# Attention weights kept in 32 bits and streamed past stationary values, two heads on the two halves of TensorE's columns

## Chip, cores and metric

One core of a Trainium2 chip. The metric is the device time of one execution, in microseconds (us). Shown for the kernel before are three runs and one profiled execution, which has a time of its own.

## What is computed

Clustered attention, then a mixture of experts. There are 4 batches, 8 heads, 768 positions, head size 64, 16 clusters per head. A query attends only to keys of its own cluster (if there is none, the row is uniform over all keys). The output of attention, 3072 tokens of 512, goes through 8 experts with hidden size 1024, whose gates are normalised over tokens and experts eight times.

```
mask   = argmax_c(q_n . c_n) == argmax_c(k_n . c_n)
scores = where(mask, q k^T / 8, -1e9)
attn   = exp(scores - max);  attn = attn / (sum(attn) + 1e-9)
x      = attn v                                 # 3072 x 512
out    = sum_e P[:, e] * (relu(x w1[e]) w2[e])  # P from x w_gate
```

## The kernel before

Attention comes first, for 32 heads in 16 pairs; the expert layers follow and take most of the time. Inside attention there is no fixed loop. Each piece of work is a generator (`load_pair`, `split_part`, `assign_pair`, `max_chunk`, `max_rows`, `exp_chunk`, `values`, `out_pair`, `out_batch`), which yields what it waits for (an event, or a token that stands for a buffer) and, before each operation, an engine and a planned cost in us. `Planner.run` (L123) picks at each step among the ready pieces by their earliest start and their urgency (`KEYS`, L385), and the order of instructions on every engine is thereby fixed when the program is built. Where a step gives two engines with costs, the planner picks one. An instruction that takes longer on the chip than planned delays what was put behind it on its engine.

A head is 768 keys by 768 queries, with the keys along the partitions, in nine chunks of 512 score columns (`CHUNKS`, L181): for each pair of key tiles two chunks of one key tile and 512 queries and one chunk of both key tiles and the last 256 queries.

- `split_part` (L555) and `assign_pair` (L591) transpose q and k of two heads on TensorE, split them in a high and a low part and work out the clusters; `place_pair` (L660) moves halves between partitions by DMA.
- `max_chunk` (L695): one matmul for a rough score of 512 columns into one of two PSUM banks (`max_ps`), and VectorE's maximum over it (L714), 9 a head. `max_rows` (L720) takes the maximum of a row, splits its negative in two fp32r parts on VectorE (L728 to L737), transposes them on TensorE (L741), and writes them by SP's DMAs as two rows beside q, from where the next matmul subtracts them; a third part, `nh`, marks rows that have no key.
- `exp_chunk` (L761): two matmuls give 512 score columns in one of three banks (`exp_ps`); ScalarE takes the exponential into `pe`, 32 bits (L794). `pe` is then split for the next product: a cast to f16 `ph` on ScalarE or VectorE (L798, L800), and the rest `pl = pe - ph` in f16, nearly always on GpSimd (L802).
- `load_group` (L451) loads the values of four heads. It finds their largest magnitude (L469 to L493), scales and splits them in f16 parts `vh` (with a column of ones) and `vl` (L503, L505), and sums them over all keys for the rows without a key (L518 to L541).
- `values` (L806), one head at a time: `ph` and `pl` are the stationary operand, 128x128, and the 64 or 65 columns of `vh`, `vl` are streamed. There are three matmuls for each key tile and query tile, 108 a head, and six with 2 rows for the rows without a key (L836). The output has queries on the partitions, and its 65th column is the denominator. Three VectorE steps normalise it (L843 to L851); the accumulator is one PSUM bank.
- `out_pair` (L860) transposes the output of two heads on TensorE (L872) and copies it with a scale on ScalarE (L876) into `xT`, the layout that the expert layers read. `out_batch` (L882) stores it and forms the gate logits in 32 bits on three column strips of TensorE (L901).

A plain fp32 matmul is recorded as two MATMULs (two passes); fp32r is one pass. The line that the change replaces in `values`:

```
nc.tensor.matmul(av[:, i, :], ph, vh[:, j, :], ...)
nc.tensor.matmul(av[:, i, 0:D], ph, vl[:, j, :], ...)
nc.tensor.matmul(av[:, i, :], pl, vh[:, j, :], ...)
```

Of the kernel before, what the change touches and what calls it, by code (L numbers as in the profile page):

```python
# [8 lines left out]
F32 = mybir.dt.float32  # L9
# [11 lines left out]
P = 128  # L21
# [131 lines left out]
def attn_moe_kernel(  # L153
# [23 lines left out]
    PB = 5  # L177
# [130 lines left out]
    with ExitStack() as actx:  # L308
# [5 lines left out]
        ps_s = actx.enter_context(tc.tile_pool(name="ps_s", bufs=3, space=PSUM))  # L314
# [44 lines left out]
        for nm, ts in bufs.items():  # L359
            if "X" in nm:  # L360
                for t in ts:
                    nc.gpsimd.memset(t[64:128, :].bitcast(F32), 1.0 if nm[0] == "k" else 0.0)
# [12 lines left out]
        for i in range(3):  # L375
            nc.vector.memset(mm[i].bitcast(F32), 0.0)
# [54 lines left out]
        t_x, t_s, t_m, t_v = Tokens(2), Tokens(3), Tokens(2), Tokens(1)  # L431
        t_nat, t_sc, t_pe, t_ph, t_nh, t_vn = Tokens(2), Tokens(1), Tokens(5), Tokens(PB), Tokens(3), Tokens(1)

# [17 lines left out]
        def load_group(n):  # L451
# [3 lines left out]
            if n >= 2 * G:  # L455
                yield ev["v", n - G - 1]
                yield ev["out", n // 2 - G + 1]
# [8 lines left out]
            am4 = sm.tile([P, G], F32, name="am4")  # L466
            for i in range(G):
                yield DVE, 0.469
                nc.vector.tensor_reduce(  # L469
                    out=am4[:, i : i + 1], in_=vn[:, i].rearrange("p t d -> p (t d)"), axis=AX, op=ALU.max, apply_absolute_value=True  # L470
                )
            yield DVE, 0.073
            am = sm.tile([P, 1], F32, name="am")
            nc.vector.tensor_reduce(out=am, in_=am4, axis=AX, op=ALU.max)
            yield t_x
            yield PE, 0.13, 0.107, 0.1
            ps = misc_tile()
            nc.tensor.transpose(out=ps[0:1, 0:P], in_=am, identity=ident)
            yield DVE, 0.198
            gm = sm.tile([1, 1], F32, name="gm")  # L480
            nc.vector.tensor_reduce(out=gm, in_=ps[0:1, 0:P], axis=AX, op=ALU.max)
            yield DVE, 0.069
            nc.vector.tensor_scalar(out=gm, in0=gm, scalar1=float(2.0**-100), scalar2=None, op0=ALU.max)
            yield DVE, 0.069
            nc.vector.tensor_single_scalar(out=gm.bitcast(I32), in_=gm.bitcast(I32), scalar=0x7F800000, op=ALU.bitwise_and)
            yield PE, 0.14, 0.053, 0.01
            nc.tensor.matmul(ps[:, 0:1], ones[0:1, :], gm, start=True, stop=True)
            yield DVE, 0.065
            vinv = sm.tile([P, 1], F32, name="vinv")
            nc.vector.tensor_scalar(out=vinv, in0=ps[:, 0:1], scalar1=float(2.0**-12), scalar2=None, op0=ALU.mult)  # L490
            vs = sm.tile([P, 1], F32, name="vs")
            yield DVE, 0.075
            nc.vector.reciprocal(vs, vinv)  # L493
            t_x.put(plan)
            if n:
                plan.now.key = urgency("vsplit", n)
            yield POOL, 0.106
            vh = work.tile([P, G, NT, D + 1], F16, name="vh")
            vl = work.tile([P, G, NT, D], F16, name="vl")
            nc.gpsimd.memset(vh[:, :, :, D : D + 1], 1.0)  # L500
            for i in range(G):
# [3 lines left out]
                nc.vector.scalar_tensor_tensor(  # L505
                    out=vl[:, i], in0=vn[:, i], scalar=vs, in1=vh[:, i, :, 0:D], op0=ALU.mult, op1=ALU.subtract
                )

            if n:
                plan.now.key = urgency("vsum", n)  # L510
            elif GATES[2]:
                yield ev["rows", 0]
            vsum = None
            for i in range(1, NT):
# [6 lines left out]
            t_vn.put(plan)  # L521
# [3 lines left out]
            nc.tensor.matmul(ps[0:2, 0 : G * D], ones[:, 0:2], vsum.rearrange("p h d -> p (h d)"), start=True, stop=True)  # L525
            yield DVE, 0.39
            ms = sm.tile([2, G, D], F32, name="ms", bufs=1)
            nc.vector.tensor_scalar(
                out=ms.rearrange("p h d -> p (h d)"), in0=ps[0:2, 0 : G * D], scalar1=vs[0:2, :], scalar2=1.0 / S, op0=ALU.mult, op1=ALU.mult
            )  # L530
            t_x.put(plan)
            yield DVE, 0.6
            mh = sm.tile([2, G, D], F16, name="mh", bufs=1)
            nc.vector.tensor_copy(mh, ms)
            mh2 = sm.tile([2, G, D], F32, name="mh2", bufs=1)
            nc.vector.tensor_scalar(out=mh2, in0=mh, scalar1=sgn, scalar2=None, op0=ALU.mult)
            yield DVE, 0.67
            ve = sm.tile([2, G, D + 1], F16, name="ve")
            nc.vector.scalar_tensor_tensor(out=ve[:, :, 0:D], in0=ms, scalar=row, in1=mh2, op0=ALU.mult, op1=ALU.add)
            for i in range(G):  # L540
                nc.vector.tensor_copy(ve[:, i, D : D + 1], first)  # L541
            t.update(vh=vh, vl=vl, ve=ve, vinv=vinv)
# [152 lines left out]
        def max_chunk(n, c):  # L695
# [7 lines left out]
            if n not in heads:  # L703
                heads[n] = dict(views(n), mr=sm.tile([P, NT, 2], F32, name="mr", bufs=3))
# [15 lines left out]
        def max_rows(n):  # L720
# [5 lines left out]
            nm = sm.tile([P, NT], F32, name="nm")  # L726
            mr = sm.tile([P, NT], F32, name="mr1")
            nc.vector.tensor_reduce(out=mr, in_=t["mr"], axis=AX, op=ALU.max)  # L728
            yield DVE, 0.072
            nc.vector.tensor_scalar(out=nm, in0=mr, scalar1=-BIG / 2, scalar2=-1.0, op0=ALU.max, op1=ALU.mult)  # L730
            yield DVE, 0.072
            nc.vector.tensor_copy(m_[:, 0:NT], nm)
            plan.now.engine = None
            yield DVE, 0.072
            nc.vector.tensor_scalar(out=m_[:, 2 * NT : 3 * NT], in0=mr, scalar1=-BIG / 2, scalar2=None, op0=ALU.is_lt)
            yield DVE, 0.075
            nc.vector.tensor_tensor(out=m_[:, NT : 2 * NT], in0=nm, in1=m_[:, 0:NT].bitcast(F32), op=ALU.subtract)  # L737
# [18 lines left out]
            t["nh"] = nh = sm.tile([2, S], F32, name="nh", bufs=3)  # L756
            for j in range(2):
                nc.sync.dma_start(out=nh[j : j + 1, :].rearrange("o (t p) -> o t p", p=P), in_=mt[2 * NT : 3 * NT, :])
            ev["nh", n].set(plan, plan.copied(0.02))

        def exp_chunk(n, c):  # L761

            u = c // 3
# [4 lines left out]
            if c % 3:  # L768
                yield ev["unit", n, u]
            else:  # L770
                yield t_ph
# [6 lines left out]
            if c % 3 == 0:  # L778
                t["ph", u] = work.tile([P, 2, S], F16, name="ph", bufs=PB)
                t["pl", u] = work.tile([P, 2, S], F16, name="pl", bufs=PB)  # L780
                ev["unit", n, u].set(plan)
# [24 lines left out]
        def values(n):  # L806
# [6 lines left out]
            for c in range(NCH):  # L813
                yield ev["p", n, c]
                if c == NCH - 2:
                    yield ev["nh", n]
# [520 lines left out]
```

## Time and profile before

| | |
|---|---|
| three runs, us | 2541.73, 2542.37, 2546.51 |
| the profiled execution, us | 2536.28 |
| its span, first to last instruction | 2534.5 |
| mean granted TensorE clock | 0.974 of full speed |
| busy over the span | TensorE 95%, VectorE 58%, ScalarE 37%, GpSimd 26% |

Busy shares over the span mix attention with the expert layers, so the trace is read by stretches. TensorE's records overlap, because matmuls are pipelined: the distance from one start to the next tells what a matmul occupies, not its duration. In the rows an arrow stands between a tile and what it is computed from, and "<-DVE mr L714" at the end of a row names what ended the idle time before it. DVE is VectorE, ACT ScalarE, POOL GpSimd, PE TensorE.

### The profile page before, as it was taken

How to read it: one execution, taken by the hardware profiler on the slowest of the kernel's cores; microseconds unless marked ns; L12 is line 12 of the kernel's file. 1: busy time of each engine (PE TensorE's matmuls, PEld its weight loads, DVE VectorE, ACT ScalarE, POOL GpSimd, SP SyncE). 2: the span in 40 equal slices, each digit the busy share in tenths (PEclk: the TensorE clock that was granted, in tenths of full speed). 3: DMA queues.
4: the chain of work that ended last, by engine and by line, in shares of the span. 5: the costliest groups of instructions: out<-in, count | busy, mean ns of one | idle time of the engine just before them, and what ended most of it. 6: DMA issues, size and time to landing. Idle time of an engine off the chain costs nothing.

```text
span 2534.5 us, 38588 instructions
## 1 busy us (share of the span) xinstructions
PE 2401.7 (95%) x15528; PEld 1371.1 (54%) x15528; DVE 1474.1 (58%) x2704; ACT 942.5 (37%) x1748; POOL 669.8 (26%) x583
## 2 busy tenths in 40 slices
PE   7988899887898999999999999999999999999999
PEld 4766677664444545455545455555555555555554
DVE  8999899998775554444444446544444434434444
ACT  5776677665424242424333322222222221221221
POOL 5777567665505050504232300000000000000000
PEclk8999899989898999999999999999999999999999
DMA  8454354416877453425243313332232222232332
GB/s 185 102 118 105 83 120 96 121 43 239 292 258 236 149 189 111 150 100 171 95 156 117 123 71 110 119 113 92 95 111 92 98 108 92 101 105 92 103 111 89
DMA packets 154708, 320.68 MB, mean 127 GB/s; under 512 B 61088, under 2 KB 90528, under 8 KB 154016
## 3 DMA queue, kind: packets, MB, share of 16 engines
q1 hardware_dynamic: 154528, 318.21, 39.9%
q8 instruction: 122, 2.00, 0.3%
q14 instruction: 58, 0.48, 0.1%
HBM read 230.74 MB, written 58.72 MB: 114 GB/s over the span
## 4 chain that ended last, share of the span: by engine, by line
PE 67%; DVE 16%; POOL 6%; DMA 5%; issue 4%; ACT 2%; SPq 0%; POOLq 0%; ACTq 0%; DVEq 0%
PE h_ps L1140 28%; PE o_ps L1202 10%; PE o_ps L1203 10%; PE o_ps L1204 10%; DVE mr L714 4%; POOL r L1060 2%; DMA r<-in_moe_w 2%; DMA scan<-in_moe_w 2%; PE max_ps L710 2%; POOL wa L1072 1%; POOL wb L1069 1%; DVE am L286 1%; PE exp_ps L787 1%; PE av_ps L830 1%; PE exp_ps L788 1%
## 5 line engine op out<-in xcount | busy, mean ns | idle before, releaser
L1140 PEld LDWEIGHTS <-wa 128*128 128x128 f16 x5376 | 527.6, 98 | 468.4 <-issue 47.0
L1152 DVE SCALAR_TENSOR_TENSOR hl<-c,hh 128x384 f16<-128x384 f32 x512 | 316.8, 619 | 537.7 <-ACT hh L1151 537.2
L1140 PE MATMUL h_ps<-xsT,wa 128*128 128x384 f16 x3072 | 586.1, 327 | 12.6 <-DVE u L1162 6.0
L1204 PE MATMUL o_ps<-wb,hl 128*128 128x512 f16 x1536 | 583.6, 380 | 7.7 <-DVE hl L1152 7.7
L1151 ACT ACTIVATE hh<-c 128x384 f16<-128x384 f32 x512 | 267.0, 522 | 857.4 <-DVE c L1162 853.7
L1202 PE MATMUL o_ps<-wb,hh 128*128 128x512 f16 x1536 | 584.3, 380 | 0.0
L1203 PE MATMUL o_ps<-wb,hh 128*128 128x512 f16 x1536 | 584.0, 380 | 0.0
L1140 PE MATMUL h_ps<-xsB,wa 128*128 128x384 f16 x2304 | 424.2, 328 | 17.0 <-DVE c L1162 14.9
L802 POOL TENSOR_TENSOR pl<-pe,ph 128x512 f16<-128x512 f32 x270 | 337.1, 1269 | 155.3 <-ACT ph L800 86.9
L1204 PEld LDWEIGHTS <-hl 128*128 128x128 f16 x1536 | 150.7, 98 | 189.1 <-DVE hl L1152 9.6
L1162 DVE SCALAR_TENSOR_TENSOR c<-h_ps,u 128x384 f32<-128x384 f32 x256 | 141.9, 554 | 181.8 <-PE h_ps L1140 180.8
L1162 DVE SCALAR_TENSOR_TENSOR u<-h_ps,m 128x384 f32<-128x384 f32 x256 | 141.8, 554 | 158.2 <-PE h_ps L1140 157.8
L1202 PEld LDWEIGHTS <-hh 128*128 128x128 f16 x1536 | 150.8, 98 | 141.1 <-issue 1.7
L1203 PEld LDWEIGHTS <-hh 128*128 128x128 f16 x1536 | 150.9, 98 | 140.2 <-issue 2.1
L1167 ACT ACTIVATE c<-h_ps 128x384 f32<-128x384 f32 x128 | 62.4, 488 | 414.1 <-PE h_ps L1140 414.0
L794 ACT ACTIVATE pe<-exp_ps 128x512 f32<-128x512 f32 x288 | 168.6, 600 | 92.7 <-PE exp_ps L788 85.9
L714 DVE TENSOR_REDUCE mr<-max_ps 128x1 f32<-128x512 f32 (+1 forms) x288 | 190.9, 677 | 16.9 <-PE max_ps L710 15.9
L710 PE MATMUL max_ps<-kX,qX 96*128 96x256 f32 (+1 forms) x384 | 130.3, 406 | 36.6 <-DVE mr L714 35.4
L1064 POOL TENSOR_TENSOR wa<-r,wa 128x256 f16<-128x256 f32 (+1 forms) x62 | 58.8, 967 | 393.6 <-ACT wa L1063 393.6
L1222 DVE SCALAR_TENSOR_TENSOR acc<-o_ps,gates,acc 128x512 f32<-128x512 f32 x168 | 125.3, 746 | 44.1 <-PE o_ps L1204 44.1
L800 ACT CAST ph<-pe 128x512 f16<-128x512 f32 x242 | 145.2, 623 | 2.6
L830 PE MATMUL av_ps<-vh,ph 128*128 128x65 f16 x1152 | 141.9, 200 | 4.1 <-DVE xn L851 4.1
(196 smaller groups left out, 2713.3 us busy)
## 6 DMA issues: line engine op xcount, KB each, us to landing
wa<-wd SPq DMA_DIRECT2D x96, 896.0 KB
wb<-wd SPq DMA_DIRECT2D x96, 512.0 KB
r<-in_moe_w SPq DMA_DIRECT2D x64, 512.0 KB
wd<-wa SPq DMA_DIRECT2D x32, 896.0 KB
scan<-in_moe_w SPq DMA_DIRECT2D x56, 512.0 KB
wd<-wb SPq DMA_DIRECT2D x32, 512.0 KB
qn<-in_q SPq DMA_DIRECT2D x16, 384.0 KB
kn<-in_k SPq DMA_DIRECT2D x16, 384.0 KB
```

What stands on the lines that cost most here:

```text
L710: nc.tensor.matmul(ps[:, y * (z - a) : (y + 1) * (z - a)], t["qa"][0:96, i * P : (i + 1) * P], t["k2"][0:96, a:z], start=True, stop=True)
L714: nc.vector.tensor_reduce(out=t["mr"][:, i0 : i0 + ni, ni - 1], in_=ps.rearrange("p (x c) -> p x c", x=ni), axis=AX, op=ALU.max)
L794: nc.scalar.activation(pe, ps.rearrange("p (x c) -> p x c", x=ni), AF.Exp, scale=SCALE)
L802: (nc.vector if e == DVE else nc.gpsimd).tensor_tensor(out=pl, in0=pe, in1=ph, op=ALU.subtract)
L830: nc.tensor.matmul(av[:, i, :], ph, vh[:, j, :], start=begin, stop=False, skip_group_check=True)
L1140: nc.tensor.matmul(ps[:, 0:HB], wa[:, w_, a, c, :], x[:, x_, c, :], start=(first and s_ == 0), stop=(s_ == len(steps) - 1), skip_group_che ...
L1151: nc.scalar.activation(hh[:, 2 - i, o], src, AF.Relu)
L1152: nc.vector.scalar_tensor_tensor(out=hl[:, 2 - i, o], in0=src, scalar=0.0, in1=hh[:, 2 - i, o], op0=ALU.max, op1=ALU.subtract)
L1162: nc.vector.scalar_tensor_tensor(out=t, in0=ps[:, 0:HB], scalar=KAPPA, in1=x, op0=ALU.mult, op1=ALU.add)
L1202: nc.tensor.matmul(po[i], hh[:, t, ti], wbh[:, t], start=(first and t == 0), stop=False)
L1203: nc.tensor.matmul(po[i], hh[:, t, ti], wbl[:, t], start=False, stop=False)
L1204: nc.tensor.matmul(po[i], hl[:, t, ti], wbh[:, t], start=False, stop=(last and t == 1))
```

## The change

The weights `pe` are no longer split. `values` works on a pair of heads: the stationary operand is a key tile of plain fp32 values, 128 keys by 64, and the weights move past it, 512 columns at a time. The first head's product lands in partitions 0 to 63 of the accumulator, the second's in 64 to 127, by way of the two halves of TensorE's columns. The output is therefore already transposed: `out_pair` goes. The denominator comes from sums of the weights over the key tiles, added on GpSimd or VectorE as the chunks appear (`t["sum"]`), and a matmul by ones that spreads the column sums over each head's 64 partitions; VectorE takes the reciprocal of 512 and 256 columns and multiplies. The accumulator takes two PSUM banks, still one buffer; the score banks go from three to two; the 32-bit weights have 14 buffers in place of 5 (the f16 parts had 5 of their own). The values' scale and f16 split go. The row steps behind the maximum move to one copy on ScalarE and two operations on GpSimd; the sign of the rows kept beside k changes with them. Constants and buffers are filled once at the start.

```diff
@@ buffers
-    PB = 5
+    PB = 14
-        ps_s = actx.enter_context(tc.tile_pool(name="ps_s", bufs=3, space=PSUM))
+        ps_s = actx.enter_context(tc.tile_pool(name="ps_s", bufs=2, space=PSUM))
-        t_x, t_s, t_m, t_v = Tokens(2), Tokens(3), Tokens(2), Tokens(1)
+        t_x, t_s, t_m, t_v = Tokens(2), Tokens(2), Tokens(2), Tokens(1)
...
@@ load_group
-            vn = nat.tile([P, G, NT, D], F32, name="vn", bufs=1)
+            vn = nat.tile([P, G, NT, D], F32, name="vn", bufs=2)
...
-            for i in range(G):
-                yield ACT, 0.507
-                nc.scalar.activation(vh[:, i, :, 0:D], vn[:, i], AF.Copy, scale=vs)
-                yield DVE, 0.529
-                nc.vector.scalar_tensor_tensor(
-                    out=vl[:, i], in0=vn[:, i], scalar=vs, in1=vh[:, i, :, 0:D], op0=ALU.mult, op1=ALU.subtract
-                )
...
@@ max_rows
-            nc.vector.tensor_scalar(out=nm, in0=mr, scalar1=-BIG / 2, scalar2=-1.0, op0=ALU.max, op1=ALU.mult)
-            nc.vector.tensor_copy(m_[:, 0:NT], nm)
-            nc.vector.tensor_scalar(out=m_[:, 2 * NT : 3 * NT], in0=mr, scalar1=-BIG / 2, scalar2=None, op0=ALU.is_lt)
-            nc.vector.tensor_tensor(out=m_[:, NT : 2 * NT], in0=nm, in1=m_[:, 0:NT].bitcast(F32), op=ALU.subtract)
+            yield ACT, 0.19
+            nc.scalar.copy(m_[:, 0:NT], mr)
+            yield POOL, 0.1
+            nc.gpsimd.tensor_scalar(out=m_[:, 2 * NT : 3 * NT], in0=mr, scalar1=-BIG / 2, scalar2=None, op0=ALU.is_le)
+            nc.gpsimd.tensor_tensor(out=m_[:, NT : 2 * NT], in0=mr, in1=m_[:, 0:NT].bitcast(F32), op=ALU.subtract)
...
@@ exp_chunk
-            if (yield (ACT, 0.52, RELUCT[0]), (DVE, 0.335, RELUCT[1])) == DVE:
-                nc.vector.tensor_copy(ph, pe)
-            else:
-                nc.scalar.copy(ph, pe)
-            e = yield ((DVE, 0.6, RELUCT[2]), (POOL, 1.113)) if n >= nheads - NL else (POOL, 1.113)
-            (nc.vector if e == DVE else nc.gpsimd).tensor_tensor(out=pl, in0=pe, in1=ph, op=ALU.subtract)
...
+            for part in parts:
+                if a not in old:
+                    old[a] = part
+                    continue
+                n_ = z - a
+                e = yield (POOL, 0.06 + n_ * 0.0023), (DVE, 0.08 + n_ * 0.00104, RELUCT[2])
+                (nc.gpsimd if e == POOL else nc.vector).tensor_tensor(out=st[:, a:z], in0=old[a], in1=part, op=ALU.add)
+                old[a] = st[:, a:z]
...
@@ values, for a pair p of heads
+            for c in range(NCH):
+                for x in range(2):
+                    yield ev["p", n + x, c]
+                yield PE, 0.87, 0.107, 0.43
+                if c == 0:
+                    av = ps_v.tile([P, 1024], F32, name="av_ps")
+                i0, ni, a, z = CHUNKS[c]
+                for i in range(i0, i0 + ni):
+                    for t, vn, o in two:
+                        nc.tensor.matmul(
+                            av[o, a:z], vn[:, i, :], heads[t]["pe", c][:, i - i0], start=(i == 0), stop=False, skip_group_check=True
+                        )
...
+            for a, z in SPANS:
+                nc.tensor.matmul(av[:, a:z], ve, nh[0:4, a:z], start=False, stop=True, skip_group_check=True)
...
+            for a, z in SPANS:
+                yield t_x
+                yield PE, (z - a) * 0.0021, 0.107, 0.11
+                ps = misc_tile()
+                for t, vn, o in two:
+                    nc.tensor.matmul(ps[o, 0 : z - a], ones[:, 0:D], heads[t]["sum"][:, a:z], start=True, stop=False, skip_group_check=True)
+                nc.tensor.matmul(
+                    ps[:, 0 : z - a], one5.rearrange("p x d -> p (x d)"), nh[:, a:z], start=False, stop=True, skip_group_check=True
+                )
+                yield DVE, 0.08 + (z - a) * 0.00104
+                ri = work.tile([P, z - a], F32, name="ri", bufs=2)
+                nc.vector.reciprocal(ri, ps[:, 0 : z - a])
+                t_x.put(plan)
+                yield DVE, 0.08 + (z - a) * 0.00104
+                nc.vector.tensor_tensor(out=xts[b][:, h // 2, a:z], in0=av[:, a:z], in1=ri, op=ALU.mult)
...
@@ order of the scores: the two heads of a pair in turn
-                plan.spawn(exp_chunk(n, c), urgency("exp", n, c))
+                plan.spawn(exp_chunk(n, c), urgency("exp", n // 2 * 2, 2 * c + n % 2))
```

## Rows read from the trace of the kernel before

Columns of the first group: stretch in us, its length, then busy us and instructions of TensorE, its weight loads, VectorE, ScalarE and GpSimd, TensorE's granted clock as a share of full speed, DMA share and GB/s. In a list by line: engine, operation, tiles, shapes and count, then busy us and mean ns, then the idle time before them and what ended it. In a timeline: start in us, duration in us, engine, line, operation.

**Rows 1.** Busy time by stretch, steady attention and the expert layers:
```profile
100.00:500.00 400.00, 357.48 (x4044) 277.68 (x4044) 374.53 (x758) 284.02 (x560) 265.50 (x228) 0.94 0.45 107
...
590.00:2534.00 1944.00, 1889.43 (x9996) 980.87 (x9995) 933.74 (x1627) 537.90 (x967) 282.64 (x242) 0.99 0.38 131
```

**Rows 2.** VectorE by line, 100 to 500 us:
```profile
L714 DVE TENSOR_REDUCE mr<-max_ps 128x1 f32<-128x512 f32 (+1 forms) x214 | 142.0, 677 | 12.9 <-PE max_ps L710 12.2
```

**Rows 3.** Timeline of TensorE, 330 to 338 us:
```profile
330.49 0.40 PE L787 MATMUL exp_ps<-qL,kH 128*128 128x512 f32 x1
330.73 0.40 PE L788 MATMUL exp_ps<-qX,kX 98*128 98x512 f32 x1
...
331.75 0.19 PE L830 MATMUL av_ps<-vh,ph 128*128 128x65 f16 x1
...
333.99 0.19 PE L832 MATMUL av_ps<-vh,pl 128*128 128x65 f16 x1
334.12 0.20 PE L836 MATMUL av_ps<-ve,nh 2*128 2x65 f16 x1
...
336.07 0.39 PE L787 MATMUL exp_ps<-qL,kH 128*128 128x256 f32 x1
```

**Rows 4.** Timeline of all engines, 300 to 308 us, a maximum on TensorE:
```profile
304.70 0.50 PE L710 MATMUL max_ps<-kX,qX 96*128 96x512 f32 x1 [2.61 <-DVE mr L714]
```

**Rows 5.** The same timeline, two additions on VectorE and GpSimd's work:
```profile
299.08 3.94 POOL L802 TENSOR_TENSOR pl<-pe,ph 128x512 f16<-128x512 f32 x3
...
300.62 1.39 DVE L518 TENSOR_TENSOR vsum<-vsum,vn 128x256 f32<-128x256 f32 x1
...
303.57 0.41 DVE L518 TENSOR_TENSOR vsum<-vsum,vn 128x256 f32<-128x256 f32 x1
```

**Rows 6.** VectorE by line and shape, 0 to 720 us, groups that go:
```profile
L798 DVE CAST ph<-pe 128x512 f16<-128x512 f32 x46 | 31.6, 689 | 3.1 <-ACT pe L794 3.1
...
L505 DVE SCALAR_TENSOR_TENSOR vl<-vn,vs,vh 128x384 f16<-128x384 f32 x32 | 23.1, 723 | 2.3 <-ACT vh L503 2.3
...
L802 DVE TENSOR_TENSOR pl<-pe,ph 128x512 f16<-128x512 f32 x18 | 20.2, 1138 | 0.1
L851 DVE TENSOR_TENSOR xn<-av_ps,rs 128x384 f32<-128x384 f32 x32 | 17.6, 550 | 0.4
L469 DVE TENSOR_REDUCE am<-vn 128x1 f32<-128x384 f32 x32 | 17.0, 538 | 0.0
L730 DVE TENSOR_SCALAR nm<-mr 128x6 f32<-128x6 f32 x32 | 15.1, 470 | 0.1
L737 DVE TENSOR_TENSOR mm<-nm,mm 128x6 fp32r<-128x6 f32 x32 | 13.9, 435 | 0.0
L732 DVE CAST mm<-nm 128x6 fp32r<-128x6 f32 x32 | 13.7, 428 | 0.0
```

**Rows 7.** The same view, reciprocals:
```profile
L845 DVE RECIPROCAL rs<-rs 128x6 f32<-128x6 f32 x32 | 5.9, 184 | 0.6
...
L1004 DVE RECIPROCAL rsum<-rsum 128x24 f32<-128x24 f32 x8 | 2.3, 293 | 0.1
```

**Rows 8.** Timeline of TensorE, 211 to 212.55 us, cluster scores:
```profile
211.85 0.51 PE L606 MATMUL misc_ps<-qn,cm 128*32 128x384 f32 x1
211.85 0.51 PE L606 MATMUL misc_ps<-kn,cm 128*32 128x384 f32 x1
...
212.19 0.49 PE L606 MATMUL misc_ps<-qn,cm 128*32 128x384 f32 x1
```

**Rows 9.** Timeline of TensorE, 212.5 to 214.8 us, gate scores:
```profile
212.52 1.90 PE L901 MATMUL misc_ps<-xT,wg 128*32 128x256 f32 x24
214.35 0.50 PE L710 MATMUL max_ps<-kX,qX 96*128 96x512 f32 x1
```

**Rows 10.** GpSimd and ScalarE by line and shape, 0 to 720 us:
```profile
L802 POOL TENSOR_TENSOR pl<-pe,ph 128x512 f16<-128x512 f32 x270 | 337.1, 1269 | 155.3 <-ACT ph L800 86.9 <-DVE ph L798 25.6 <-issue 19.4
...
L800 ACT CAST ph<-pe 128x512 f16<-128x512 f32 x242 | 145.2, 623 | 2.6
```

More of the change, by code (lines that the diff above doesn't have):

```diff
@@ L475, in load_group @@
[L475 to L496, printed above, removed]
@@ L509, in load_group @@
[L509 to L512, printed above, removed]
+            plan.now.key = urgency("vsum", n)
             vsum = None
@@ L520, in load_group @@
                 )
-            t_vn.put(plan)
             yield t_x
@@ L524, in load_group @@
             ps = misc_tile()
[L525 to L529, printed above, removed]
-            )
[L531 to L542, printed above, removed]
+            nc.tensor.matmul(ps[0:4, 0 : G * D], ones[:, 0:4], vsum.rearrange("p h d -> p (h d)"), start=True, stop=True)
+            yield DVE, 0.4
+            ms = sm.tile([4, G * D], F32, name="ms", bufs=1)
+            nc.vector.tensor_tensor(out=ms, in0=ps[0:4, 0 : G * D], in1=halves.rearrange("p h d -> p (h d)"), op=ALU.mult)
+            t_x.put(plan)
+            yield ACT, 0.4
+            mh = sm.tile([4, G * D], F32R, name="mh", bufs=1)
+            nc.scalar.copy(mh, ms)
+            yield DVE, 0.3
+            mh2 = sm.tile([4, G * D], F32, name="mh2", bufs=1)
+            nc.vector.tensor_scalar(out=mh2, in0=mh.bitcast(F32), scalar1=sgn4, scalar2=None, op0=ALU.mult)
+            yield DVE, 0.4
+            ve = sm.tile([4, G, D], F32R, name="ve")
+            nc.vector.scalar_tensor_tensor(
+                out=ve.rearrange("p h d -> p (h d)"), in0=ms, scalar=odd, in1=mh2, op0=ALU.mult, op1=ALU.add
+            )
+            t.update(vn=vn, ve=ve)
             ev["group", b, g].set(plan)
@@ L703, in max_chunk @@
             if n not in heads:
-                heads[n] = dict(views(n), mr=sm.tile([P, NT, 2], F32, name="mr", bufs=3))
+                heads[n] = dict(views(n), mr=mrs[n % 4])
             t = heads[n]
@@ L810, in values @@
             yield ev["group", b, h // G]
[L811 to L820 removed]
+            gr = groups[(b, h // G)]
@@ new lines, in values @@
+                plan.spawn(release(p, c), plan.now.key)
+            for x in range(2):
+                yield ev["nh", n + x]
+            yield PE, 0.34, 0.107, 0.11
+            for a, z in SPANS:
+                nc.tensor.matmul(av[:, a:z], ve, nh[0:4, a:z], start=False, stop=True, skip_group_check=True)
+            if h % G == G - 2:
+                t_vn.put(plan)
+            if h == 0:
+                if b:
+                    yield ev["batch", b - 1]
+                xts[b] = sm.tile([P, NC, S], F32, name="xT", bufs=1)
@@ L865, in out_pair @@
+            for x in range(2):
+                yield ev["s", n + x, NCH - 1]
             for a, z in SPANS:
                 yield t_x
-                yield PE, 0.12 * (z - a) / P, 0.107, 0.107
-                if h == 1 and a == 0:
-                    xts[b] = sm.tile([P, NC, S], F32, name="xT", bufs=1)
+                yield PE, (z - a) * 0.0021, 0.107, 0.11
                 ps = misc_tile()
-                for i in range(a // P, z // P):
-                    nc.tensor.transpose(out=ps[:, i * P - a : (i + 1) * P - a], in_=xn[:, i, :], identity=ident)
@@ L882, in out_batch @@
+            for x in range(2):
+                t_nh.put(plan)
+                t_sum.put(plan)
+                ev["v", n + x].set(plan)
+            t_v.put(plan)
+            if p + 1 < npairs:
+                plan.spawn(values(p + 1), urgency("values", 2 * p + 2))
+            if h == H - 2:
+                plan.spawn(out_batch(b), urgency("batch", n + 1))
+        xts = {}
         def out_batch(b):
```

152 lines of the change are left out of this document (56 added, 96 removed).

## The prediction

> **What bounds the kernel now.** I read the stretches first. The change touches only attention, the first 590 us of a span of 2534.5 us; the 1944 us behind it are the expert layers, which it leaves alone [rows 1]. Within attention the 400 us from 100 to 500 are steady: VectorE is busy 94%, TensorE 89%, ScalarE 71%, GpSimd 66%, and TensorE's granted clock averages 0.94 [rows 1]. The pace comes from the row maxima: one head has 9 of these reductions, a pair of heads 18, and 214 of them in 400 us are 11.9 pairs, so 33.6 us a pair [rows 2]. VectorE is at work 374.5 / 11.9 = 31.5 us of that.
>
> TensorE's 89% needs care, since matmul records overlap. Counted by starts, a 512-column matmul on fp32r data takes 0.24 us [rows 3]. A chunk needs one such matmul for the maximum and two for the scores: 18 x 0.72 = 13.0 us a pair. The values of one head are 108 weight loads of 128x128 f16, each with 64 or 65 columns, and 6 corrections; 96 of them and the corrections run from 331.75 to 336.07 [rows 3], 4.3 us, and with the other 12 it is 4.7, or 9.4 a pair. Six output transposes are some 0.7, and the transposes and cluster scores at the front of a pair about 3 (an estimate: 12 transposes at 0.12 from the 0.24 row, a cluster round of 0.67, the rest small). Sum 26.1 us: TensorE streams for 78% of the pace. What it loses is waiting, such as the 2.61 us before a maximum whose bank VectorE had not yet emptied [rows 4], and the lower of its two clock levels (1.2 GHz instead of 2.4), which the average of 0.94 contains. So **VectorE is the bound and TensorE follows.**
>
> VectorE is slow partly because of GpSimd: the same sum of values took 1.39 us while GpSimd was working through three subtractions, which end at 303.02, and 0.41 us after them, at 303.57 [rows 5]. Some of the groups below are slow for the same reason.
>
> **What leaves VectorE.** From [rows 6], whole attention: the f16 cast of weights 31.6, the weights' low parts 20.2, the values' low parts 23.1, the values' maxima 17.0, the normalisation 17.6, three of the small row steps 15.1 + 13.7 + 13.9; from [rows 7] the old reciprocals 5.9. Together 158 us, 9.9 a pair. A dozen smaller groups that go too are left as a margin.
>
> **What comes to VectorE.** The output is now transposed, so every one of the 64 lanes of a head holds the denominator of each query, and the reciprocal runs over 512 and 256 columns instead of 6. Does a reciprocal cost by its columns? 6 columns took 184 ns, 24 took 293 [rows 7]: (293 - 184) / 18 = 6.1 ns a column. 512 columns are then 3.3 us, 256 columns 1.7, 5.0 us a pair, or 80 us in all. The planner's costs in the diff are 0.61 and 0.35. The other bound, if the slope belonged to short operations alone, is 1.4 ns a column (550 ns for the 384 columns of the normalisation [rows 6]), 1.1 a pair; I take the slope, since it is measured on the same operation. The Trainium skill (VectorE: DVE Perf Modes, "First, the fixed hardware budget" and "Specifications") says that the divide repeats 8 times and that the clock is 0.96 GHz. An estimate by that page is 8.3 ns a column and 6.4 us a pair, which would make the sum 1.4 us a pair worse; no run here shows it. The slope above is the lower of the two, and it is the measured one. The new multiplications cost 2 x 0.55 = 1.1 a pair [rows 6]. The key-tile sums are 20 additions a pair, half of 512 and half of 256 columns; GpSimd's cost carries no penalty in the diff, and VectorE did 18 of 288 of the old subtractions [rows 6], so about 20 of 320, some 1 us each beside GpSimd, 1.3 a pair (bounds 0 and 4). The values' mean correction keeps about the same count of small operations. Sum 7.4.
>
> VectorE: 31.5 - 9.9 + 7.4 = **29.0 us a pair.**
>
> **TensorE.** Removed: 9.4 + 0.7 = 10.1. Added: per chunk, two heads times 512 columns of plain fp32, which goes in two passes. Do the halves of the columns run side by side? Products of 384 columns on neighbouring column strips start at the same 211.85, and the second passes 0.34 us later [rows 8]; 24 records, 12 products of 256 columns in threes, end before 214.35, so a round of three takes 0.43 [rows 9]. Strips do run together, and 512 columns cost 0.86 to 0.91; with 0.88, nine chunks are 7.9 a pair. Each change of the array's shape costs too: the 2-row correction starts 0.13 after its neighbour, where 75 matmuls of one shape before it start within 2.24 us, 0.03 apart [rows 3], and 0.11 passes after the strips [rows 9]. I take 0.1 a change; score matmuls stand between most chunks, so 9 x 2 x 0.1 = 1.8 (0 if all chunks came in runs). The correction: 768 columns of fp32r, 0.36, plus 0.2. The denominators: ones by the sums, 768 x 2 passes, 1.3, the 5-row term 0.36, and 0.6 for shapes. Sum 12.5. TensorE: 26.1 - 10.1 + 12.5 = **28.5 us a pair**, 2.4 more than before.
>
> **The others.** GpSimd's 337 us of subtractions [rows 10] turn into 160 additions of 512 columns and 160 of 256, at 1.27 and half of that about 306 us, less what VectorE takes, plus four small row operations a pair: unchanged, and it goes on holding up VectorE. ScalarE loses 145 us of casts [rows 10] and more; it has no part in the bound, so that gains nothing directly. Its new copies of the row maxima stand behind operations of 0.6 us [rows 10]; TensorE's transpose of them waits for ScalarE, then GpSimd, where it waited for VectorE. I cost that at nothing, because three slow VectorE steps go; if GpSimd's queue (1.27 us an entry) is ahead of the row, it is 1 to 2 us a pair. The score banks go from 3 to 2: with 0.5 us of matmul against 0.6 of exponential one bank fills while the other empties, nothing. The accumulator is one for two heads, and the next pair's values wait for sums, reciprocals and products: about 11 us (last additions 3, ones 1, reciprocals 5, products 1, handovers 1). Fourteen buffers of weights hold seven chunks of each head, and at some 1.8 us a chunk the scores can go on for 25 us, so this is hidden; with half the cover it would show. SP's queue gets the same transfers. Set-up adds about a dozen small fills and constants on VectorE before the first q arrives: hidden. At the start the first group's scale and split leave VectorE (about 5 us on the path); at the end the last pair's longer chain returns about 6.
>
> **The sum.** Before, the engine at the limit reached 31.5 / 33.6 = 94%. Now two engines stand at 29.0 and 28.5 in an order fixed in advance, so each delay of one idles the other; I take 92%: 29.0 / 0.92 = 31.5, that is 2.1 us a pair less, 34 us over 16 pairs. Against the profiled execution's 2536.3 us (span 2534.5 and 1.8 around it) that makes 2502, and I say **2501**. The median of the runs shown is 2542.4, 6 us above that execution; 0.2%, or 5 us, is about what a measurement of this kernel can tell from no change. At 96% it would be 30.2 a pair and 2482, at 90% 2514: this case's own range.
>
> **Rivals.**
> **More is gained.** Reciprocals at the rate of other operations (1.1 a pair, not 5.0) and no additions on VectorE give 29.0 - 3.9 - 1.3 = 23.8; then TensorE's 28.5, with half of the shape changes saved by runs 27.6, is the bound: 27.6 / 0.94 = 29.4, 67 us gained, 2469, and down to 2440 if the removed small groups and milder waits for GpSimd count. For it: VectorE's removed groups are certain. Against it: the slope. 0.26.
> **Slower: TensorE takes over and keeps its waits.** Now it loses 33.6 - 26.1 = 7.5 us a pair. A reciprocal of 3.3 us planned as 0.6 stands in front of the reductions that empty TensorE's banks, once a pair and then a shorter one, just where [rows 4] shows a wait. If the loss stays above 33.6 - 28.5 = 5.1 us, the kernel is slower; at 6.5 it is 35.0 a pair, 22 us more, 2558; if all 7.5 stay, 36.0 and 2574. Against it: most of those waits came from a VectorE that was full, and it has now 2.5 us less to do. 0.24.
> **The halves do not run together.** The chunks then take another 7.9 and the ones 1.3: 37.7 a pair, at 95% 39.7, 98 us more, 2634. Against it stand [rows 8, 9], so only 0.03. The Trainium skill (TensorE: Matmul & The Clock Gate, "Measured speedup vs the span model") gives 2.38-fold for three strips, not three; an estimate by that is 1.26 times the chunk's price, 2.3 us a pair or 37 us more, 2538. The rows here show no such loss.
> **Nothing measurable:** the efficiency falls to 86% and the gain goes. 0.07.
>
> **Numbers.** Forecast 0.40, more 0.26, slower 0.24 and 0.03, same 0.07: faster 0.66, same 0.07, slower 0.27. The range 2440 to 2562 leaves out the far ends of both rivals.
>
> **What the profile would show.** Reciprocals near 3.3 and 1.7 us; value matmuls of the two heads starting together, 0.43 to 0.45 apart by pass, and no weight casts on ScalarE; VectorE down to about 85 to 92% and TensorE's streaming up in the steady stretch; the expert stretch unchanged at 1944 us. Wrong would be: reciprocals near 0.7; the second head's products behind the first's; waits of the maxima for VectorE longer than now; a clock lower than 0.94.

## The result, and the profile after

The changed kernel takes 2567.9 us (median of 4 runs, 2566.9 to 2568.5), the kernel before 2543.1 in the same rounds: ratio 1.0095, interval 1.0078 to 1.0113. It is slower by 25 us, where 2501 us was forecast, about 42 less than the kernel before. The profiled execution's span is 2565.1 us, 30.6 more than before. All of it lies in attention: the expert layers still fill 1945 us.

Busy time by stretch of the changed kernel, columns as in [rows 1]:

```profile
100.00:500.00 400.00, 370.49 (x1886) 207.89 (x1884) 304.09 (x452) 173.11 (x347) 263.70 (x290) 0.92 0.43 101
...
620.00:2565.00 1945.00, 1890.05 (x9996) 980.76 (x9994) 935.17 (x1626) 541.49 (x972) 287.60 (x247) 0.99 0.38 131
```

VectorE is down from 94% to 76% of the steady stretch, ScalarE from 71% to 43%; TensorE is up from 89% to 93%, and its granted clock is down from 0.94 to 0.92. The maxima give the pace, as in [rows 2]. VectorE by line, 100 to 500 us, changed kernel:

```profile
L692 DVE TENSOR_REDUCE mrt<-max_ps 128x1 f32<-128x512 f32 (+1 forms) x202 | 133.7, 680 | 69.4 <-PE max_ps L688 68.6
```

202 / 18 = 11.2 pairs in 400 us, 35.6 us a pair instead of 33.6, and 16 times 2.0 us is about the 31 us of the span. VectorE now waits 68.6 us for TensorE's maxima, where it waited 12.2.

What came to VectorE, by line and shape, the attention stretch of the changed kernel (reciprocals, products, and the share of the key-tile sums that the planner gave it):

```profile
L836 DVE RECIPROCAL ri<-misc_ps 128x512 f32<-128x512 f32 x16 | 53.7, 3354 | 16.1 <-PE misc_ps L831 16.1
L836 DVE RECIPROCAL ri<-misc_ps 128x256 f32<-128x256 f32 x16 | 28.0, 1750 | 5.7 <-PE misc_ps L831 5.7
...
L839 DVE TENSOR_TENSOR xT<-av_ps,ri 128x512 f32<-128x512 f32 x16 | 10.9, 678 | 0.1
...
L777 DVE TENSOR_TENSOR psum<-psum,pe 128x256 f32<-128x256 f32 x10 | 9.8, 985 | 5.9 <-ACT pe L758 5.8
...
L777 DVE TENSOR_TENSOR psum<-psum,pe 128x512 f32<-128x512 f32 x9 | 7.9, 878 | 11.5 <-ACT pe L758 11.5
```

The end of a pair shows how a reciprocal gets in the way. Timelines of TensorE and VectorE in the changed kernel, 300 to 323 us:

```profile
301.31 1.08 PE L830 MATMUL misc_ps<-psum,ones 128*64 128x512 f32 x4
302.32 0.49 PE L831 MATMUL misc_ps<-nht,one 5*128 5x512 f32 x1
...
308.62 0.50 PE L688 MATMUL max_ps<-kX,qX 96*128 96x256 f32 x2 [0.36 <-DVE mrt L692]
...
311.75 1.08 PE L808 MATMUL av_ps<-pe,vn 128*64 128x512 f32 x4 [0.67 <-DVE xT L839]
...
314.92 0.50 PE L751 MATMUL exp_ps<-qL,kH 128*128 128x512 f32 x1
315.26 0.40 PE L752 MATMUL exp_ps<-qX,kX 98*128 98x512 f32 x1
...
321.56 1.08 PE L808 MATMUL av_ps<-pe,vn 128*64 128x512 f32 x4
322.57 0.38 PE L751 MATMUL exp_ps<-qL,kH 128*128 128x256 f32 x1
```

```profile
303.91 3.34 DVE L836 RECIPROCAL ri<-misc_ps 128x512 f32<-128x512 f32 x1
307.28 0.69 DVE L839 TENSOR_TENSOR xT<-av_ps,ri 128x512 f32<-128x512 f32 x1
307.89 1.28 DVE L692 TENSOR_REDUCE mrt<-max_ps 128x1 f32<-128x512 f32 x2
309.08 1.75 DVE L836 RECIPROCAL ri<-misc_ps 128x256 f32<-128x256 f32 x1
```

Between 303.91 and 307.89 no maximum is taken, and from 305.2 on, when the second of TensorE's two banks for them has been written, both stay full. The four passes of a chunk, two heads side by side, occupy 1.01 us (321.56 to 322.57): 0.86 of streaming and 0.15 for two changes of shape. The first score matmul behind such a change takes 0.34 (314.92 to 315.26) instead of the 0.24 of [rows 3].

At this pair end TensorE had other work and waited only 0.36 us for a maximum's bank. At others it stands still, here 2.70 us (363 to 369 us, TensorE and then VectorE):

```profile
365.16 0.33 PE L883 MATMUL misc_ps<-ident,gt 96*128 96x96 f32 x2
368.18 0.80 PE L688 MATMUL max_ps<-kX,qX 96*128 96x256 f32 x2 [2.70 <-DVE mrt L692]
```

```profile
364.22 3.36 DVE L836 RECIPROCAL ri<-misc_ps 128x512 f32<-128x512 f32 x1 [0.47 <-PE misc_ps L831]
367.50 0.63 DVE L692 TENSOR_REDUCE mrt<-max_ps 128x1 f32<-128x512 f32 x1
```

Between 100 and 500 us TensorE waits 13 times for a maximum, 18.5 us in all. In eight of these waits, 16.3 us, the bank comes free by the first maximum behind a reciprocal.

The clock falls at the same places. Of the 400 us, TensorE had 61 at the lower clock level, in nine spells at nine of the eleven pair ends. Each spell begins during or just behind a standstill of TensorE of 1.1 to 2.8 us: seven of these were waits for a maximum, one for the accumulator (L808) and one for a bank that a reciprocal reads (L238). The other two pair ends have standstills too (2.2 and 0.75 us) and no spell. The spell that follows the rows above, in the columns of [rows 1]:

```profile
368.20:371.60 3.40, 3.40 (x10) 2.57 (x10) 2.07 (x5) 1.33 (x3) 1.92 (x3) 0.50 0.00 0
```

**One account for all kernels.** The columns of the stretch 100 to 500 us give TensorE's budget. Pairs are maxima / 18 (in the table's order 214, 202, 219, 233, 206, 212, 207 and 221 maxima). Idle is 400 less TensorE's busy time. A granted share of 0.92 means that 8% of 400 us, 32 us of full-speed time, was lost to the lower of the two clock levels (1.2 and 2.4 GHz; a stretch at the lower one is granted 0.50). What is left, busy less clock loss, divided by the pairs, is what a pair needs of TensorE at full clock; the share is given to 0.01, so the need is known to about 0.2 us, and what the clock lost while TensorE was idle anyway is counted twice.

| kernel | pairs | idle, us | clock loss, us | need per pair, us |
|---|---|---|---|---|
| before | 11.9 | 42.5 | 24 | 28.0 |
| changed | 11.2 | 29.5 | 32 | 30.2 |
| one pass (e1) | 12.2 | 50.3 | 56 | 24.1 |
| no division (e2) | 12.9 | 8.8 | 0 | 30.2 |
| early free (e3) | 11.4 | 25.1 | 24 | 30.7 |
| true cost (e5) | 11.8 | 21.8 | 16 | 30.7 |
| runs of three (e7) | 11.5 | 38.8 | 32 | 28.6 |
| true cost and runs (e10) | 12.3 | 19.2 | 16 | 29.7 |

Before, a pair took 28.0 of need and 5.6 of loss (42.5 + 24 over 11.9). After, 30.2 of need and 5.5 of loss. **The work on TensorE grew by 2.2 us a pair and the loss did not shrink.** Its make-up changed: idle time went from 3.6 to 2.6 us a pair, and clock loss from 2.0 to 2.9. TensorE waits less for the maxima than before (28.5 us in this stretch then, 18.5 now), but most of what is left of them stands at the pair ends, where the clock falls. This row is of the kernel before, TensorE's waits in 100 to 500 us (total, times, longest):

```profile
PE max_ps L710 <- DVE mr L714: 28.5, 26, 4.7
```

The experiments ask where the need and the loss come from. The changed kernel ran only in its first rounds; the differences to it below are of medians. By the ratios to the kernel before, which ran in every round, some gains come out up to 5 us smaller: 26 us and not 29 for e5, 6 and not 9 or 10 for e6 and e7.

### The profile page after: what moved, and what is told of

Read it like the earlier page. It is cut to its first block, busy times and chain, and to the rows that moved or that the text cites. A ratio compares the mean times of both kernels' runs of the same rounds, so it can differ in the third digit from the quotient of the medians.

```text
span 2565.1 us, 32392 instructions
## 1 busy us (share of the span) xinstructions
PE 2438.1 (95%) x12720; PEld 1281.4 (50%) x12720; DVE 1401.9 (55%) x2349; ACT 807.5 (31%) x1493; POOL 674.8 (26%) x679
## 4 chain that ended last, share of the span: by engine, by line
PE 76%; DVE 9%; POOL 6%; issue 4%; DMA 3%; ACT 1%; SPq 0%; POOLq 0%; ACTq 0%; DVEq 0%
PE h_ps L1110 28%; PE o_ps L1174 11%; PE o_ps L1172 11%; PE o_ps L1173 11%; PE av_ps L808 5%; PE max_ps L688 3%; PE exp_ps L751 3%; DVE ri L836 2%; PE exp_ps L752 2%; POOL r L1030 2%; DMA r<-in_moe_w 2%; DVE mrt L692 2%; POOL wa L1042 2%; DVE am L286 1%; DMA scan<-in_moe_w 1%
## 5 line engine op out<-in xcount | busy, mean ns | idle before, releaser
L777 POOL TENSOR_TENSOR psum<-psum,pe 128x512 f32<-128x512 f32 (+1 forms) x237 | 251.5, 1071 | 123.1 <-ACT pe L758 116.4
L692 DVE TENSOR_REDUCE mrt<-max_ps 128x1 f32<-128x512 f32 (+1 forms) x288 | 189.8, 680 | 91.9 <-PE max_ps L688 91.0
L808 PE MATMUL av_ps<-pe,vn 128*64 128x512 f32 (+1 forms) x768 | 153.0, 510 | 8.8 <-DVE xT L839 8.8
L752 PE MATMUL exp_ps<-qX,kX 98*128 98x256 f32 (+1 forms) x384 | 134.5, 361 | 0.0
```

What stands on the lines that cost most here:

```text
L692: nc.vector.tensor_reduce(out=t["mr"][:, i0 : i0 + ni, ni - 1], in_=ps.rearrange("p (x c) -> p x c", x=ni), axis=AX, op=ALU.max)
L752: nc.tensor.matmul(o, t["k2"][0:98, ki], t["qa"][0:98, a:z], start=False, stop=True)
L777: (nc.gpsimd if e == POOL else nc.vector).tensor_tensor(out=st[:, a:z], in0=old[a], in1=part, op=ALU.add)
L808: nc.tensor.matmul(av[o, a:z], vn[:, i, :], heads[t]["pe", c][:, i - i0], start=(i == 0), stop=False, skip_group_check=True)
```

## The experiments

**e1, one pass.** Weights and values of the value product are read as bf16 through a view.

```diff
-    av[o, a:z], vn[:, i, :], heads[t]["pe", c][:, i - i0], ...
+    av[o, a:z], vn.bitcast(BF16).rearrange("p t (d u) -> p t d u", u=2)[:, i, :, 1],
+    heads[t]["pe", c].bitcast(BF16).rearrange("p n (s u) -> p n s u", u=2)[:, i - i0, :, 1], ...
```

> Leaves out the lower 16 bits of weights and values in the value product (both are read as bf16 through a view), so each product takes one pass instead of two; nothing else changes, and the planned costs stay, so the order does too. Theory A, TensorE's own work is the new bound (two passes, 0.86 us a chunk): 0.64 x 144 chunks = 92 us of TensorE go, and most of it shows, 60 to 90 us: 2478 to 2508. Theory B, the gap between two pairs (values stand still until sums, reciprocals and products have emptied the one accumulator): the gap of some 11 us a pair stays, only the dense part between gaps shrinks until VectorE or ScalarE binds: 20 to 50 us, 2518 to 2548.

Measured 2524.9 us, ratio to before 0.9929 (0.991 to 0.9948), so 43 us less than the changed kernel, inside the range of theory B; whether its gap is the accumulator's is asked by e3. Busy time by stretch of this kernel:

```profile
100.00:500.00 400.00, 349.75 (x1733) 209.72 (x1731) 338.22 (x490) 187.34 (x377) 285.94 (x315) 0.86 0.47 108
```

The need falls by 6.1 us a pair, as much as nine chunks at 0.64 (5.8) and the clock's rounding allow. (For 512 columns of both heads a recorded pass of plain fp32 occupies 0.43 us and the bf16 pass 0.22, so one pass in place of two takes away three quarters of the 0.86.) But idle and clock loss rise to 106 us, 8.7 a pair. Of 92 us of TensorE work that were taken away, about half came back as waiting and as lower clock: work alone is not what sets the pace.

**e2, no division.** `nc.vector.reciprocal(ri, ps)` becomes `nc.vector.tensor_copy(ri, ps)`.

> Leaves out the division: the reciprocal is replaced by a copy of the same shape, order unchanged. The reciprocals of 3.35 and 1.75 us become 0.7 and 0.4, 4.0 us a pair off VectorE, 64 us in all. Theory A: VectorE has slack (76% busy in the steady stretch), so under 10 us: 2558 to 2568. Theory B: the gap shrinks by 4 us in every pair and TensorE loses less to the low clock: 40 to 65 us, 2503 to 2528.

Measured 2501.4 us, ratio 0.9837 (0.9818 to 0.9855), 66 us less than the changed kernel: theory B, 2 us beyond its range, though what shrinks most is the wait for the maxima. Busy time by stretch, and who waited for whom on TensorE in 100 to 500 us, without the division:

```profile
100.00:500.00 400.00, 391.21 (x2126) 216.99 (x2124) 307.72 (x517) 197.37 (x397) 303.84 (x329) 1.00 0.47 110
```

```profile
PE misc_ps L714 <- POOL mm L710: 4.7, 5, 1.4
PE max_ps L688 <- DVE mrt L692: 3.1, 9, 0.8
```

The same view of the changed kernel:

```profile
PE max_ps L688 <- DVE mrt L692: 18.5, 13, 2.8
PE av_ps L808 <- DVE xT L839: 3.7, 3, 1.9
```

The waits of the maxima go from 18.5 us to 3.1, the clock stays at full but for one spell of 3.4 us, and the need is the same 30.2. So the division takes nearly the whole loss of a pair with it, although VectorE had a quarter of its time free. Here TensorE is busy 98% of the stretch, and a pair takes 30.9 us, close to the 30.2 that TensorE's work needs.

**e3, early free.** The accumulator is copied out at once and released.

```diff
+            ao = work.tile([P, S], F32, name="ao", bufs=1)
+            for a, z in SPANS:
+                yield ACT, 0.09 + (z - a) * 0.00098
+                nc.scalar.copy(ao[:, a:z], av[:, a:z])
+            t_v.put(plan)
+            if p + 1 < npairs:
+                plan.spawn(values(p + 1), urgency("values", 2 * p + 2))
```

> ScalarE copies the accumulator to SBUF (about 0.7 and 0.4 us) as soon as the last product is in, and the next pair's values may start; sums, reciprocals and the product follow from the copy. Nothing of the computation is left out. Theory A: TensorE's work is the same, so 0 to 10 us either way: 2558 to 2578. Theory B: the values no longer stand still at the end of a pair; TensorE is fed there and keeps its clock: 30 to 65 us less, 2503 to 2538, below the kernel before.

Measured 2562.7 us, ratio 1.0077 (1.0056 to 1.0098): 5 us less than the changed kernel. Theory B falls in the form in which I had it: TensorE no longer waits for the products (3.7 us before, none now), and the time hardly moves. TensorE's waits for VectorE, 100 to 500 us, early free:

```profile
PE max_ps L688 <- DVE mrt L692: 16.3, 12, 2.5
PE misc_ps L837 <- DVE ri L843: 3.0, 2, 1.5
```

The maxima still wait 16.3 us, 12.7 of them directly behind a reciprocal. What costs most is not the accumulator but what stands behind a reciprocal in VectorE's queue.

**e4, the row steps alone, on the kernel before.** `max_rows`, the sign of the rows and the prefilled maxima are taken from the change; the rest is the kernel before.

> The kernel before with one part of the change alone: the row steps behind the maximum move from VectorE (470 + 428 + 191 + 435 ns a head) to one ScalarE copy and two GpSimd operations. If VectorE bounds the kernel before, as its 94% says, 48 us of it go and 20 to 40 show: 2503 to 2523. If the longer way through ScalarE's and GpSimd's queues (entries of 0.6 and 1.3 us) delays the transpose of the rows, on which TensorE already waited 15.6 us, it is the same or up to 15 us slower: 2543 to 2558.

Measured 2550.4 us, ratio 1.0035 (1.0021 to 1.005). It is slower by 7 us in the median, but it doesn't answer the question, because the planner spent part of what was freed. VectorE by line, 100 to 500 us, this kernel:

```profile
L796 DVE CAST ph<-pe 128x512 f16<-128x512 f32 x43 | 29.1, 688 | 2.6 <-ACT pe L792 2.6
```

There are 43 casts of weights on VectorE in the 400 us; the kernel before has 27. VectorE is busy 368.9 of the 400 us. Whether VectorE bounded the kernel before is left open by this run; that this part of the change brings nothing by itself, in this planner's order, is shown.

**e5, true cost.** The planned cost of a reciprocal becomes `0.16 + (z - a) * 0.00624`.

> Only the planner's cost of a reciprocal changes, from 0.61 and 0.35 us to the measured 3.35 and 1.75, so that the fixed order puts other work around it. Theory C, the plan is wrong: TensorE needs about 31.5 us a pair at full clock, and what it loses beyond that comes from maxima queued behind reciprocals that last 4 us longer than planned, and from the low clock after those waits. Then 30 to 60 us of the 66 that the division costs come back: 2508 to 2538. Theory D, VectorE's time itself is short at the end of a pair, whatever the order: within 10 us of the changed kernel, 2558 to 2568.

Measured 2538.7 us, ratio 0.9992 (0.9979 to 1.0005): 29 us less than the changed kernel with the same operations, by theory C (0.7 us outside its range). Busy time by stretch, and TensorE's first wait in the same stretch:

```profile
100.00:500.00 400.00, 378.16 (x1997) 211.38 (x1994) 318.53 (x476) 189.08 (x377) 273.29 (x302) 0.96 0.46 108
```

```profile
PE max_ps L688 <- DVE mrt L692: 4.8, 7, 1.6
```

The wait of the maxima falls to 4.8 us, and the clock rises to 0.96; the need is 30.7, 0.5 more, at the edge of its error. So 29 of the 66 us come back when one planned cost is put right. That the price alone does it is not shown: a new price gives a new order all through attention, and e6 is an order with right prices that gains little.

**e6, true cost in pieces of 128 columns.** Six reciprocals of 128 columns, planned at 0.95 us each, in place of the two.

> The reciprocals are cut into pieces of 128 columns, planned at 0.95 us each, so that maxima can go between them; VectorE's sum rises by some 1 us a pair (four more starts). Theory C with the head of the queue as the cause: at least as good as the true cost alone, 2500 to 2535. Theory D: 2558 to 2585.

Measured 2558.5 us, ratio 1.0072 (1.0054 to 1.0091), 9 us less than the changed kernel and 20 more than e5: a miss for theory C, at the lower edge of theory D's range. A piece took 942 ns, as planned, so the price was right; the maxima waited 20.0 us again over the attention stretch (5.5 in e5). In 100 to 500 us:

```profile
PE max_ps L688 <- DVE mrt L692: 18.6, 20, 3.0
```

The trace shows behind what. Of these 18.6 us, 7.3 stand behind pieces of a reciprocal, where 16.3 stood behind whole ones in the changed kernel. The other 11.3 stand behind other work of VectorE, mostly the splits of q and k (L564, L566), up to 1.7 us each. Why this order puts them there was not looked into.

**e7, runs of three.** The value products of three chunks are issued together, planned at 3 x 0.87 us.

> The value products of three chunks are issued together, so TensorE goes to the half-column shape and back three times a pair instead of up to nine. If each round trip costs 0.35 us (0.86 us of streaming, 1.01 to the next start, and the score matmul behind it 0.34 instead of 0.24) and TensorE is the bound throughout, six fewer are 2.1 us a pair, 34 us: 2534 to 2550. If the stretches behind the reciprocals decide, or the longer runs starve ScalarE and VectorE, nothing: 2558 to 2578.

Measured 2557.9 us, ratio 1.0073 (1.0058 to 1.0088): 10 us less, at the edge of the second expectation. Busy time by stretch:

```profile
100.00:500.00 400.00, 361.17 (x1913) 213.13 (x1912) 337.59 (x473) 171.93 (x347) 258.66 (x283) 0.92 0.44 101
```

The need falls by 1.6 us a pair, to 28.6, but idle time rises from 29.5 to 38.8 us.

**e8, exp(-ln x) on ScalarE.**

```diff
-                nc.vector.reciprocal(ri, ps[:, 0 : z - a])
+                nc.scalar.activation(ri, ps[:, 0 : z - a], AF.Ln)
+                nc.scalar.activation(ri, ri, AF.Exp, scale=-1.0)
```

> The reciprocal is taken on ScalarE as exp(-ln x), two operations of the same shape, and VectorE only multiplies; nothing of the computation is left out. Both theories C and D: VectorE is rid of 5.1 us a pair, ScalarE gains about 2.2 and was idle for 57%: 2495 to 2515, as without the division. If logarithm and exponential don't share a loaded table, there are some 64 table loads of 1.28 us each (as the one row of the trace has it), in the way of the exponentials: 2520 to 2580.

Measured 2566.4 us, ratio 1.0109 (1.0092 to 1.0127): no gain, inside the range for functions that don't share a table. VectorE is rid of the division, and ScalarE pays for it. ScalarE by line, attention stretch:

```profile
L839 ACT ACT_TABLE_LOAD x32 | 41.1, 1283 | 0.6
L842 ACT ACT_TABLE_LOAD x19 | 24.4, 1283 | 0.3
L758 ACT ACT_TABLE_LOAD x14 | 18.0, 1283 | 0.4
```

65 table loads are 83 us on ScalarE, in front of the exponentials: TensorE waits 29.2 us for `pe` over the attention stretch, 0.8 in the changed kernel.

```profile
PE exp_ps L751 <- ACT pe L758: 29.2, 25, 2.2
```

The Trainium skill (ScalarE: Activation LUTs, "Table sets: the hidden batching unit") names a set that holds both functions and would need one load; this run has 65 loads for 32 logarithms, and the run decides.

**e9, no division and runs of three.**

> Leaves out the division (a copy in place of the reciprocal) and issues the value products in runs of three chunks. Without the division TensorE ran at full clock for all but 3.4 of 400 us and stood still for under 4 us of the stage, at 31.6 us a pair. Theory E, what I counted too low on TensorE is the change of shape: six round trips of 0.35 us fewer a pair are 2.1 us, 34 us in all: 2464 to 2480 against 2501. Theory F, the rest is elsewhere (denominators, transposes, handovers), or longer runs starve the other engines: 2492 to 2510.

Measured 2496.8 us, ratio 0.9816 (0.9799 to 0.9832), 4.7 us below e2. Theory F: with TensorE full, runs of three save little. By the account above its row (382.70 busy, clock 1.00, 233 maxima) gives a need of 29.6, 0.6 less than e2, and 17.3 us of idle time instead of 8.8. (The 31.6 us a pair and the standstill of under 4 us that the expectation names for e2 are 30.9 and 8.8 by its row above.) The changes of shape are a small term, and what runs save in this stretch comes back as waits.

**e10, true cost and runs of three.** Both edits, nothing left out.

> The true planned cost of the reciprocals and runs of three chunks together, nothing left out. If both gains add (29 and 10 us against the changed kernel): 2525 to 2533, below the kernel before. If runs of three only filled the time that the wrong plan left idle: 2535 to 2545.

Measured 2529.9 us, ratio 0.995 (0.9932 to 0.9969). It beats the kernel before by 0.5% and the changed kernel by 38 us, about the sum of the two single gains (29 and 10; by the ratios 37 against 26 and 6). Busy time by stretch:

```profile
100.00:500.00 400.00, 380.77 (x2030) 217.42 (x2026) 333.60 (x483) 188.27 (x378) 285.52 (x315) 0.96 0.45 106
```

**e11, true cost, casts of q and k always on ScalarE.** `RELUCT[5]` 0.05 to 1.0, `RELUCT[4]` 0.2 to 0.

> The true planned cost of the reciprocals, and the high parts of q and k always cast on ScalarE (busy 43%) instead of VectorE, where these casts are 19 us in all and wait for GpSimd. If VectorE's work around the reciprocals still costs TensorE something: 5 to 15 us below the true cost alone, 2524 to 2534. If TensorE's own 31.6 us a pair is all that is left: 2534 to 2544.

Measured 2536.8 us, ratio 0.9983 (0.997 to 0.9996), 2 us from e5: the second expectation. VectorE's further relief (309 us busy in the stretch instead of 319) brings nothing that can be told from noise here.

**e12, a nudge.** The planned cost of the exponential in the changed kernel goes from 0.50 to 0.52.

> The changed kernel with one planned cost moved a little, the exponential from 0.50 to 0.52 us (measured 0.60): the same work in a slightly other order, to see how much of a difference the order alone can make. If orders hardly matter: within 4 us of 2568. If they do, 5 to 15 us either way, and differences of that size between the other kernels tell little.

Measured 2570.6 us, ratio 1.0104 (1.0087 to 1.0121), 2.7 us from the changed kernel. This one reordering moved the time by 3 us, so I read differences of 5 us between kernels (e3, e9 against e2) as no more than a hint. It is one nudge, and e5 and e6 lie 20 us apart, so an order can matter more than this. The effects of 29, 38, 43 and 66 us rest on the waits and the clock in the traces as well as on the times.

## Why the prediction was wrong

**The listed terms of VectorE were right.** The reciprocals took 3.35 and 1.75 us, 5.1 a pair where 5.0 stood; the products 1.1; 19 additions on VectorE where 20 stood. Its total came out at 304.1 / 11.2 = 27.1 us a pair, 2 below the sum of 29.0. The sum lacks a term for that: the planner gave VectorE fewer of the splits of q and k, and they were shorter there (75 operations of 64.8 us in the 400 us before, L586 and L588; 51 of 31.6 us after, L564 and L566). The small groups left as a margin go too. (The 9.9 us that the sum takes off are durations, and VectorE's records overlap: in the 400 us before they add up to 425 where it is busy 374.5, so this term was too large rather than too small.) GpSimd's additions sum to 317 us, predicted 306.

**The added work of TensorE was right, its base was not.** Predicted plus 2.4 us a pair, measured plus 2.2 (28.0 to 30.2). The base of 26.1 was counted from bare matmul starts; by the account it is 28.0, so the new need was 30.2 and not 28.5. Which work the count missed was not isolated; changes of shape around the scores are one candidate. Two halves of the columns do run together, as [rows 8] and [rows 9] had it: 1.01 us for a chunk with its changes of shape, where 0.88 + 0.2 stood. The rival of halves one after the other, and the partial overlap worked out from the Trainium skill (TensorE: Matmul & The Clock Gate, "Measured speedup vs the span model"), both fall. e7 and e9 put what six round trips cost at 0.6 to 1.6 us a pair, where 0.1 a change made 1.2.

**The step that failed is the sum.** I divided the greater of the two engine sums by 92%, as if the loss would follow the load: 31.5 a pair, that is 3.0 us of loss beside TensorE's 28.5. The loss before was 5.6 us by the account and it stayed at 5.5, so the pace went to 35.6: of the 4.1 us a pair that the prediction missed, about 2.5 are this loss and 1.7 the base. This is the rival "TensorE takes over and keeps its waits", with its place (maxima behind a reciprocal planned too short) and its point (a loss above 5.1 us a pair; counted as the prediction counts it, 35.6 less 28.5, it is 7.1 of the former 7.5). It gave 2558 to 2574, and I had put it at 0.24 on the ground that VectorE had less to do. That ground was the mistake. VectorE had less to do, and TensorE lost as much. Its waits for the maxima became fewer, so this sign of being wrong did not come; but those left are packed behind the reciprocals, and the other sign, a clock below 0.94, came with them (0.92). The order is fixed, and the plan held 0.96 us for 5.1 us of reciprocals, once in every pair. e2 shows that the division is worth 66 us, though VectorE is 76% busy; e5 shows that 29 of them come back with the planned cost put right. I had read the planned costs and the measured slope, 4 us apart, in the same paragraph, and let the difference into VectorE's sum alone.

**The covers named.** The accumulator's wait was costed at nothing, and e3 bears it out to 5 us. The two score banks in place of three were costed at nothing; in 100 to 500 us TensorE waited 0.6 us for the exponentials that empty them. That ScalarE's relief gained nothing was not tested by itself. The move of the row steps was costed at nothing; in the changed kernel the transposes of these rows (L714) waited 1.0 us in 400, where they waited 9.8 before (L741), but alone in the kernel before (e4) the edit costs 7 us.

**What VectorE's 94% meant.** I took it as the bound. e4 shows that the planner gives VectorE more casts when it is freed, and [rows 5] that the same addition took 1.39 us beside GpSimd's work and 0.41 behind it, so a high busy share was no proof. Whether it bound the kernel before is not settled here.

What is still open: e5 and e2 differ by 37 us, what the division costs with the plan right. Its 4.0 us a pair on VectorE are 64 us, so more than half of them show. In 100 to 500 us e5 has 13 us more idle time than e2 and 16 us of clock loss; no single wait leads: 4.8 us for the maxima, 3.8 for the DMA of the rows, 3.7 of transposes (L548) for a bank that a reciprocal reads. What each is worth was not isolated.

## What to carry to other kernels

Where the order on every engine is fixed in advance, price a new operation twice: by its time on the engine, and by the gap between that time and what the plan holds for it, for what is queued behind it can wait that long, also on an engine with time to spare. Count an engine's loss (idle time and clock) apart from its work, and don't assume that it shrinks with the load: here it stayed, and went only with the operation that caused the waits. In this case freeing VectorE was no gain, because TensorE, which had waited for it, got more work.

## What the runs showed that was not expected

A VectorE reciprocal costs 6.3 ns a column right up to 512 columns ((3354 - 1750) / 256), the same slope as from 6 to 24 columns. The granted clock of the steady stretch went from 0.92 to 1.00 by the removal of nothing but the division: with nearly all of the maxima's waits gone, one spell of 3.4 us at the lower level was left of nine with 61 us. Taking 92 us of TensorE's work away (e1) lowered the clock to 0.86 (16 spells, 123 us of the 400), so that a part of the gain was paid back in slower matmuls.
